# Three selection masks turned by DMA instead of TensorE, and two steps moved forward in their engines' orders

## The chip, the cores and the metric

The kernel runs on one core of one Trainium2 chip. The metric is the device time of one execution in microseconds (us); the time before is the median of three runs, 276.24 us (276.19 to 276.46). Everything else below comes from one profiled execution of the same kernel.

The engines are called by their profile names: PE (TensorE, matmuls), PEld (its weight loads), DVE (VectorE), ACT (ScalarE), POOL (GpSimd) and SP (SyncE, which issues nearly all DMAs; its queue is SPq in the profile).

## The reference

For 4 batches of 8 heads (768 positions, 64 features per head) a block-sparse attention is computed, and its output goes through a two-layer network with a tanh GELU.

```python
k_rep = k.reshape(B, H, n_blocks, block, D).mean(axis=3)          # 12 blocks of 64 keys
gate_scores = np.einsum('bhsd,bhnd->bhsn', q, k_rep)
gate_scores = np.where(causal, gate_scores, -1000000000.0)
top_idx = np.argsort(gate_scores, axis=-1)[..., -top_k:]          # top_k = 3
# a query sees its 3 best key blocks and its own block, and no later position
scores = np.where(mask, scale * (q @ k.T), -1000000000.0)
attn = softmax(scores); attn_out = attn @ v
# x: attn_out as 3072 tokens of 512 features
h = x @ w_in                                                      # 512 -> 2048
g = 0.5 * h * (1.0 + np.tanh(c * (h + 0.044715 * h * h * h)))
out = g @ w_out                                                   # 2048 -> 512
```

## The kernel before

The 32 heads are handled as 16 pairs of heads. Pairs 0 to 3 (batch 0) have their own functions; pairs 4 to 15 go one by one through the steps below. The network runs over 12 chunks of 256 tokens; a chunk needs the attention output of all four pairs of its batch, so the matmuls of earlier batches' chunks are mixed in between the attention of later pairs.

Nothing is scheduled by a planner at build time. A text, `ORDER` (lines 27 to 129), lists 1109 steps by name, and the program calls the function of each in turn. As the whole body stands under `tc.manual_schedule()` (line 162), each engine executes its own instructions in the order in which `ORDER` names them. Between engines, and for buffers that are used again, the framework puts in semaphore waits. So a change of `ORDER` matters only where two steps of the same engine, or two tiles of the same buffer, change places. The names, for pair p (written `x.p.0` with more numbers behind):

- `d.p.x` loads q, k or v (x = 0, 1, 2) by two DMAs on SP; `hn0`, `hn1` (hi_n, line 726) and `ln0`, `ln1` (lo_n, line 736) make the high and low fp16 halves of q and k; the letter behind the colon is the engine (a = ACT, v = DVE, p = POOL).
- `zqh`, `zkh`, `zql` (dma_t, line 746) turn the high q, high k and low q by a DMA transpose on SP; `c0`, `c1` (qk_copy, line 756) copy the turned halves of q and k into the operand tiles `qt` and `kt`, one for each head.
- `s` (k_sum, line 761, PE) sums the keys of each block; `b` (k_block, line 773, DVE, three instructions) makes the gate's weights of it; `g` (gate, line 787, PE) computes the gate scores; `m` (select, line 800, DVE, 14 instructions, the last at line 821) writes for each query and block 0 or a large negative number into `madd16`.
- `mt` (mask_t, line 826) turns that mask on PE: five transposes of 128 by 128 into a PSUM tile. `mc.p.0.hh` (mask_q, line 838) copies 12 rows by 640 columns of it below the q of head hh in `qt`, so that the matmul of the scores adds the mask by itself.
- `k.p.0.i` (score, line 846, PE), `x` (expo, line 859, ACT) and `a` (causal, line 877, POOL) make the six blocks of attention weights; `v` (v_copy, line 770) casts v; `p` (pv, line 887, PE) multiplies by v, and `n` (normalise, DVE, lines 673 and 677) divides.
- `zx` (x_dma, line 900), or `xt` and `xc`, turn the result into `xT`. Then `u` (up, line 947, PE), `y` (gelu, line 964, ACT), `f` (down, line 981, PE), `o` (out_c, line 999) and `w` (out_d, line 1009, a DMA on SP) are the network for a chunk.

The buffers of which the change speaks: PSUM has three wide tiles. The number behind `@` in `ORDER` names the one that a step `u`, `k` or `p` takes; the step waits until the reader of the tile before it (`y`, `x` or `n`) is done. One further PSUM tile, `small`, is shared by `s`, `g`, `mt` and `xt` in turn. In SBUF, the pool `hd` has two buffers of each tag; the tag `ql` holds the turned low q.

Of the kernel before, what the change touches and what calls it, by code (L numbers as in the profile page):

```python
# [27 lines left out]
c.m0.1 c.bi c.ident d0.0.1.0 c.e0 d0.1.0.0 c.ident16 dm24 d0.1.0.1 d0.0.0.0 d0.0.0.1 dd.1.1.0  # L28
dd.1.1.1 d0.1.3.2 d0.0.1.1 t2.0.0@0 c.e.2:a c.v.1 d0.1.1.0 d0.1.1.1 c.gate dm4 c.own r.1.1.0:a
r.1.1.1:a t2.1.1@1 d0.1.0.2 c.cg t2.1.0@2 c.e.1:p h2.0.0 s.0.0 l.0.0 dm8 c.m0.0 c.bd b.0.0 dd.0.1.0  # L30
h2.1.0 s.1.1 c.e.3:p dd.0.1.1 dd.0.2.0 g.0.0 m.0.0 mt.0.0 s.1.0 l.1.0 r.0.1.0:a r.0.1.1:p lw.in.2
c.v.0 h2.1.1 mc.0.0:a dm5 t2.0.1@0 b.1.0 l.1.1 h2.0.1 r.0.2.0:v d0.0.0.2 g.1.0 m.1.0 dm17 mt.1.0
s.0.1 mc.1.0:a dm4 l.0.1 k.0.0.0.0@2 k.0.0.1.0@1 ma.0.0.0 x.0.0.0.0 d0.1.1.2 v.1.0.0:p c.par.0
b.0.1 b.1.1 dm16 d0.0.1.2 x.0.0.1.0 a.0.0.1 g.0.1 k.0.1.0.1@0 k.1.0.0.0@2 k.1.0.1.0@1 ma.1.0.0
x.1.0.0.0 a.0.0.0 lw.out.1 x.1.0.1.0 m.0.1 dd.0.2.1 r.0.2.1:a mt.0.1 mc.0.1:v lw.in.4 g.1.1
k.0.1.1.1@2 v.0.0.1:p lw.in.5 ma.0.1.1 x.0.1.1.1 m.1.1 x.0.1.0.1 t2.0.2@1 d0.0.3.2 s.0.2 h2.0.2
a.0.1.0 dm9 v.0.1.1:a lw.in.3 d0.0.2.2 v.1.1.1:a l.0.2 a.1.0.1 v.1.0.1:p k.1.1.1.0@2 mt.1.1
mc.1.1:v v.0.0.0:p k.1.1.0.0@0 ma.1.1.0 x.1.1.1.0 a.0.1.1 p.0.0.0@1 p.0.0.2 p.0.0.3 p.0.0.1 n.0.0
dm22 d0.1.2.2 cw.in.5:v lw.in.1 v.1.1.0:p dd.1.2.0 cw.in.1:v k.1.1.0.1@2 k.1.1.1.1@1 ma.1.1.1
x.1.1.0.0 a.1.0.0 cw.in.4:v p.1.0.0@0 x.1.1.1.1 d.5.1 dd.1.2.1 dm23 v.0.1.0:p lw.out.0 x.1.1.0.1  # L40
r.1.2.0:a xt.0.0 xc.0.0:a lw.in.0 p.1.0.2 cw.in.2:p d.4.0 p.1.0.3 p.1.0.1 n.1.0 k.0.1.0.0@1
k.0.1.1.0@2 ma.0.1.0 x.0.1.0.0 a.1.1.0 p.1.1.0@0 p.1.1.1 xt.1.0 xc.1.0:v a.1.1.1 p.1.1.2 r.1.2.1:v
lw.out.5 x.0.1.1.0 cw.out.5:p d0.1.5.2 p.0.1.0@1 p.0.1.1 p.1.1.3 n.1.1 cw.in.3:v d.4.1 lw.in.6
lw.in.7 cw.out.1:a hn1.5.0:v p.0.1.3 cw.in.6:p cw.in.7:p lw.out.3 p.0.1.2 t2.1.2@2 n.0.1 s.1.2
b.1.2 xt.1.1 u.0.1.0@0 xc.1.1:a u.0.1.1 y.0.1 hn0.4.0:v xt.0.1 xc.0.1:a b.0.2 u.0.2.0@1 u.0.2.1
y.0.2 u.1.2.0@0 u.1.2.1 y.1.2 u.1.1.0@1 u.1.1.1 ln0.4.0:v zql.4.0 lw.out.2 y.1.1 d0.0.5.2
cw.out.0:a cw.in.0:v u.0.0.0@0 u.0.0.1 g.0.2 u.1.0.0@1 u.1.0.1 y.0.0 hn1.4.0:v u.0.3.0@0 m.0.2
cw.out.3:v mt.0.2 u.0.3.1 h2.1.2 l.1.2 y.1.0 dm9 ln1.4.0:v dm24 y.0.3 cw.out.2:v mc.0.2:v
k.0.2.1.0@2 k.0.2.0.0@1 ma.0.2.0 x.0.2.0.0 g.1.2 d.6.0 hn0.6.0:p x.0.2.1.0 k.0.2.0.1@0 k.0.2.1.1@1
zqh.4.0 ma.0.2.1 x.0.2.0.1 x.0.2.1.1 c.ke.0.0:p ln1.5.0:v m.1.2 mt.1.2 k.0.2.1.2@2 mc.1.2:v s.4.0  # L50
b.4.0 k.0.2.0.2@0 c0.4.0.0:a lw.out.6 ma.0.2.2 f.0.0.0 lw.out.4 lw.out.7 x.0.2.1.2 ln0.6.0:v
cw.out.7:v f.0.0.1 x.0.2.0.2 k.1.2.0.0@1 k.1.2.1.0@2 zkh.5.0 ma.1.2.0 x.1.2.1.0 zqh.6.0 cw.out.6:p
x.1.2.0.0 c.ke.0.1:v cw.out.4:p g.4.0 m.4.0 f.0.0.2 d0.0.4.2 v.0.2.0:v f.0.0.3 o.0.0:a d.5.0
k.1.2.0.1@0 k.1.2.1.1@2 ma.1.2.1 d0.1.4.2 f.0.1.0 hn0.5.0:v ln0.5.0:v x.1.2.0.1 a.0.2.0 zkh.4.0
v.0.2.1:p a.0.2.1 f.0.1.1 p.0.2.0@1 p.0.2.1 c.ke.1.0:a x.1.2.1.1 c0.4.0.1:p mt.4.0 d.6.1 v.1.2.1:p
c1.4.0.0:a mc.4.0.0:v c.par.1 p.0.2.3 p.0.2.2 n.0.2 v.1.2.0:a k.1.2.1.2@0 zqh.5.0 k.1.2.0.2@2
ma.1.2.2 f.0.1.2 x.1.2.0.2 f.0.1.3 zql.5.0 c1.4.0.1:v mc.4.0.1:v x.1.2.1.2 s.5.0 b.5.0 o.0.1:v
k.4.0.1@1 k.4.0.2@2 x.4.0.1 d.4.2 d.5.2 c1.5.0.0:v zql.6.0 a.1.2.0 p.1.2.0@0 p.1.2.1 g.5.0 m.5.0
x.4.0.2 c0.5.0.0:v a.1.2.1 p.1.2.3 c.q0.0 k.4.0.0@1 v.4.0:p f.1.0.0 x.4.0.0 xt.0.2 xc.0.2:a
k.4.0.5@2 p.1.2.2 x.4.0.5 k.4.0.3@1 x.4.0.3 a.4.0.3 hn1.6.0:v d.7.1 ln1.6.0:v a.4.0.5 mt.5.0 d.8.0  # L60
mc.5.0.0:v c0.5.0.1:p zkh.6.0 k.4.0.4@2 f.1.0.1 mc.5.0.1:v n.1.2 c0.6.0.1:v x.4.0.4 u.1.3.0@1
u.1.3.1 y.1.3 s.6.0 f.1.0.2 b.6.0 xt.1.2 w.0.0 xc.1.2:v d.7.0 c1.5.0.1:p hn1.7.0:v ln1.7.0:v
c.ke.1.1:p k.5.0.2@0 k.5.0.1@2 x.5.0.2 k.5.0.3@1 g.6.0 m.6.0 f.1.0.3 u.2.0.0@0 o.1.0:v d.8.1
u.2.0.1 d.9.0 x.5.0.3 a.4.0.4 a.4.0.2 a.4.0.0 a.4.0.1 p.4.0.0@1 x.5.0.1 a.5.0.1 hn0.7.0:v zqh.7.0
mt.6.0 mc.6.0.1:v d.6.2 p.4.0.1 w.1.0 mc.6.0.0:v n.4.0 c1.6.0.0:p y.2.0 c0.6.0.0:p k.5.0.4@2
c1.6.0.1:p f.1.1.0 f.1.1.1 ln0.7.0:v x.5.0.4 c.q0.1 hn1.8.0:v ln1.8.0:v k.5.0.5@1 k.6.0.2@0 x.6.0.2
s.7.0 b.7.0 f.1.1.2 v.5.0:v k.5.0.0@2 c0.7.0.1:v hn0.8.0:p x.5.0.5 ln0.8.0:v x.5.0.0 k.6.0.3@0
a.5.0.0 zql.7.0 zkh.7.0 zqh.8.0 s.8.0 f.1.1.3 b.8.0 x.6.0.3 o.1.1:a a.6.0.3 w.1.1 k.6.0.4@1 w.0.1
x.6.0.4 u.2.1.0@2 u.2.2.0@0 u.2.2.1 y.2.2 hn0.9.0:p g.7.0 a.5.0.4 u.2.1.1 c0.7.0.0:v y.2.1
u.2.3.0@1 m.7.0 a.6.0.4 u.2.3.1 mt.7.0 zql.8.0 y.2.3 a.5.0.2 ln0.9.0:v a.5.0.3 a.5.0.5 p.5.0.0@0  # L70
p.5.0.1 mc.7.0.0:v k.6.0.1@2 f.2.0.0 f.2.0.1 x.6.0.1 v.6.0:v d.10.0 a.6.0.1 n.5.0 k.6.0.0@1
k.6.0.5@2 f.2.0.2 c1.7.0.1:v x.6.0.5 a.6.0.5 x.6.0.0 mc.7.0.1:v c1.7.0.0:v k.7.0.5@0 k.7.0.2@2
zkh.8.0 x.7.0.5 c1.8.0.1:p g.8.0 x.7.0.2 hn0.10.0:v m.8.0 d.7.2 a.6.0.0 a.6.0.2 f.2.0.3 o.2.0:a
k.7.0.3@1 x.7.0.3 a.7.0.3 zx.5.0 c0.8.0.0:a k.7.0.0@0 p.6.0.0@2 p.6.0.1 x.7.0.0 mt.8.0 k.7.0.4@1
x.7.0.4 n.6.0 f.2.1.0 mc.8.0.0:v k.7.0.1@0 f.2.1.1 a.7.0.2 a.7.0.4 mc.8.0.1:a zx.4.0 c0.8.0.1:v
c1.8.0.0:v k.8.0.3@1 d.9.1 zqh.9.0 d.10.1 d.8.2 zql.9.0 a.7.0.0 d.11.0 x.7.0.1 a.7.0.1 v.7.0:v
k.8.0.1@2 x.8.0.1 a.7.0.5 x.8.0.3 xt.6.0 xc.6.0:v p.7.0.0@0 p.7.0.1 n.7.0 hn1.9.0:a zkh.9.0
c1.9.0.0:p hn1.10.0:v ln0.10.0:v zql.10.0 f.2.1.2 f.2.1.3 w.2.0 k.8.0.5@2 xt.7.0 x.8.0.5 k.8.0.4@1
xc.7.0:a zqh.10.0 k.8.0.2@0 u.3.3.0@2 u.3.3.1 ln1.9.0:v x.8.0.4 s.9.0 x.8.0.2 a.8.0.2 u.3.2.0@1
u.3.2.1 v.8.0:v u.4.2.0@0 u.4.2.1 b.9.0 g.9.0 ln1.10.0:v d.11.2 zkh.10.0 y.3.3 o.2.1:a y.3.2 y.4.2  # L80
d.12.0 hn0.11.0:v ln0.11.0:v a.8.0.4 u.3.0.0@2 zql.11.0 u.3.1.0@1 u.3.0.1 y.3.0 k.8.0.0@0 m.9.0
mt.9.0 mc.9.0.0:v mc.9.0.1:v u.3.1.1 u.5.1.0@2 u.5.1.1 y.3.1 d.11.1 y.5.1 s.10.0 a.8.0.5 x.8.0.0
c1.9.0.1:v c0.9.0.1:p c0.9.0.0:v k.9.0.1@1 x.9.0.1 hn0.12.0:a c1.10.0.0:v f.3.0.0 f.3.0.1 f.3.0.2
f.3.0.3 d.15.2 a.8.0.0 k.9.0.3@2 b.10.0 g.10.0 c1.10.0.1:p k.9.0.4@0 d.13.1 d.9.2 x.9.0.3 d.15.0
a.8.0.3 x.9.0.4 a.8.0.1 p.8.0.0@1 o.3.0:v m.10.0 p.8.0.1 n.8.0 u.4.0.0@2 u.4.0.1 y.4.0 k.9.0.2@0
x.9.0.2 ln0.12.0:v a.9.0.2 f.3.1.0 hn1.13.0:v ln1.13.0:v k.9.0.5@1 zqh.11.0 mt.10.0 mc.10.0.1:a
a.9.0.1 u.5.0.0@2 x.9.0.5 a.9.0.5 c0.10.0.0:v f.3.1.1 f.3.1.2 f.3.1.3 hn1.11.0:v k.9.0.0@0
mc.10.0.0:v o.3.1:a d.12.1 ln1.11.0:v x.9.0.0 a.9.0.0 u.4.1.0@1 zkh.11.0 v.9.0:v u.4.1.1 y.4.1
zx.8.0 s.11.0 a.9.0.4 c1.11.0.1:p u.4.3.0@0 u.4.3.1 d.14.2 y.4.3 a.9.0.3 u.5.0.1 y.5.0 hn0.15.0:p
b.11.0 w.2.1 c0.10.0.1:v d.10.2 zqh.12.0 g.11.0 k.10.0.3@1 x.10.0.3 f.4.0.0 k.10.0.1@0 x.10.0.1  # L90
c1.11.0.0:v k.10.0.5@2 m.11.0 f.4.0.1 hn1.12.0:v zkh.12.0 f.4.0.2 p.9.0.0@1 a.10.0.3 ln0.15.0:v
p.9.0.1 n.9.0 mt.11.0 k.10.0.4@0 x.10.0.4 d.13.0 mc.11.0.1:v mc.11.0.0:a f.4.0.3 v.11.0:v
c0.11.0.1:p u.5.2.0@1 ln1.12.0:v k.10.0.2@0 o.4.0:a x.10.0.5 u.5.2.1 k.10.0.0@2 x.10.0.2 zql.12.0
s.12.0 w.4.0 u.5.3.0@0 u.5.3.1 a.10.0.5 y.5.2 y.5.3 a.10.0.2 c1.12.0.0:a f.4.1.0 c0.11.0.0:p
v.10.0:v k.11.0.0@1 f.4.1.1 a.10.0.4 b.12.0 g.12.0 f.4.1.2 f.4.1.3 hn0.13.0:v x.10.0.0 a.10.0.0
x.11.0.0 d.12.2 k.11.0.1@0 x.11.0.1 k.11.0.2@2 m.12.0 mt.12.0 zx.9.0 c0.12.0.1:v o.4.1:v x.11.0.2
a.10.0.1 p.10.0.0@1 ln0.13.0:v p.10.0.1 n.10.0 zqh.13.0 c1.12.0.1:v f.5.0.0 k.11.0.3@0 zkh.13.0
k.11.0.4@2 c0.12.0.0:v v.14.0:a d.13.2 k.11.0.5@1 f.5.0.1 x.11.0.3 a.11.0.0 f.5.0.2 zql.13.0
# [985 lines left out]
```

## Time and profile before

| | |
|---|---|
| median of three runs | 276.24 us |
| the profiled execution | 278.32 us, of which 276.6 us are the span from its first to its last instruction |
| granted TensorE clock | 0.994 |
| busy, PE | 263.3 us, 95% of the span |
| busy, ACT / DVE / POOL | 198.2 / 141.4 / 86.9 us |
| transposes of masks on PE (line 830) | 60 for pairs 4 to 15, 219 ns each, overlapping |
| DMA transposes on SP (lines 751 and 903) | 36 + 8 |

Two things are needed to read it. Matmuls overlap, so the distance from one start to the next is shorter than the duration of one: what PE spends on a group is best read from the start of that group to the start of the next. And the profile shows an idle time only where no work of the engine is recorded; as the matmul before still counts as busy for a moment, a wait of PE can be some 0.15 us longer than the idle time given.

### The profile page before, as it was taken

Reading aid. Unit: us, or ns where it says so; the run is one execution under the profiler, and the core shown is the slowest. Engines: PE = TensorE matmul, PEld = TensorE weight load, DVE = VectorE, ACT = ScalarE, POOL = GpSimd, SP = SyncE. Lnnn points to the kernel's source line nnn. Section 1 sums busy time; section 2 is a strip of 40 time slices with the busy share of each in tenths; the row PEclk is TensorE's granted clock in tenths of the full one; section 3 lists DMA queues with packets and bytes.
Section 4 is the critical chain, followed back from the end, with each engine's and each line's share of the span. In section 5 each row is a group of like instructions: output and inputs, shape, how many; then the busy total and the mean of one; then the engine's idle time right before and its main releaser. Section 6 shows DMA issues by size and latency. Waiting matters only on the chain.

```text
span 276.6 us, 6874 instructions
## 1 busy us (share of the span) xinstructions
PE 263.3 (95%) x2785; PEld 183.1 (66%) x2785; DVE 141.4 (51%) x442; ACT 198.2 (72%) x229; POOL 86.9 (31%) x159
## 2 busy tenths in 40 slices
...
GB/s 173 279 329 282 252 270 295 276 170 180 175 248 192 177 199 190 185 200 213 148 212 118 188 119 114 101 135 157 79 7 23 97 0 2 0 76 2 76 92 138
DMA packets 114416, 42.66 MB, mean 154 GB/s; under 512 B 102992, under 2 KB 107344, under 8 KB 114384
## 3 DMA queue, kind: packets, MB, share of 16 engines
...
q8 instruction: 22, 0.36, 0.7%
q14 instruction: 10, 0.08, 0.1%
...
## 4 chain that ended last, share of the span: by engine, by line
PE 70%; DVE 8%; DMA 7%; ACT 7%; issue 4%; POOL 2%; SPq 1%; POOLq 0%; ACTq 0%
PE hps L957 23%; PE ops L993 20%; PE st L852 7%; PE pv L894 4%; DMA io<-in_k_dram 4%; PE pso L993 3%; PE dm L1032 3%; ACT at L868 2%; DMA qhT<-hn 2%; DMA io<-in_q_dram 2%; PE st L598 2%; DVE ln L739 2%; ACT L868 1%; PE pv L662 1%; PE st L616 1%
## 5 line engine op out<-in xcount | busy, mean ns | idle before, releaser
L957 PE MATMUL hps<-xT,w_in 128*128 128x256 f16 x768 | 90.1, 272 | 0.0
L957 PEld LDWEIGHTS <-w_in 128*128 128x128 f16 x768 | 74.0, 98 | 12.5 <-DVE xn L677 0.2
L993 PE MATMUL ops<-w_out,gT 128*128 128x512 f16 (+1 forms) x352 | 81.9, 371 | 0.0
L868 ACT ACTIVATE at<-st 128x1024 f16<-128x1024 f32 (+1 forms) x72 | 62.8, 918 | 11.1 <-PE st L852 10.8
L967 ACT ACTIVATE gT<-hps 128x1024 f16<-128x1024 f32 x48 | 48.1, 1024 | 23.0 <-PE hps L957 22.8
L993 PEld LDWEIGHTS <-gT 128*128 128x128 f16 x400 | 37.0, 97 | 36.2 <-issue 0.5
L882 POOL TENSOR_SCALAR_AFFINE_SELECT at<-at 128x256 f16<-128x256 f16 x72 | 31.1, 451 | 76.4 <-ACT at L868 66.6
L852 PE MATMUL st<-qk 76*128 76x128 f16 (+2 forms) x192 | 35.6, 306 | 0.5 <-ACT at L868 0.5
L739 DVE SCALAR_TENSOR_TENSOR ln<-io,hn 128x768 f16<-128x768 f32 x24 | 25.3, 1059 | 0.3
L635 ACT ACTIVATE at<-st 128x768 f16<-128x768 f32 (+1 forms) x24 | 20.7, 913 | 6.5 <-PE st L616 4.9
L852 PEld LDWEIGHTS <-qk 76*128 76x128 f16 x192 | 16.5, 97 | 10.8 <-issue 0.9
L1006 DVE COPY w_o<-pso 128x512 f32<-128x512 f32 x1 | 0.7, 692 | 36.9 <-PE pso L993 36.9
L894 PEld LDWEIGHTS <-at 128*128 128x128 f16 x504 | 17.1, 97 | 2.5 <-issue 0.6
L894 PE MATMUL pv<-v,at 128*128 128x65 f16 x504 | 17.7, 193 | 0.6 <-POOL v L771 0.6
L1006 ACT COPY osb<-ops 128x512 f32<-128x512 f32 (+1 forms) x13 | 7.3, 562 | 14.8 <-PE ops L993 12.8
L187 POOL TENSOR_SCALAR hn<-io 128x768 f16<-128x768 f32 x6 | 13.0, 2160 | 9.2 <-PE hps L957 5.1
L1032 PE MATMUL dm<-zsrc 128*128 128x512 f16 (+3 forms) x45 | 13.4, 431 | 2.0 <-POOL zsrc L235 2.0
L673 DVE RECIPROCAL zrec<-pv 128x12 f32<-128x12 f32 x12 | 2.8, 232 | 22.6 <-PE pv L894 22.4
L967 ACT ACT_TABLE_LOAD x11 | 14.1, 1283 | 0.2
L839 DVE COPY qk<-mt 12x640 f16<-12x640 f16 x19 | 9.2, 485 | 7.9 <-ACT qk L839 4.3
L648 POOL TENSOR_SCALAR_AFFINE_SELECT at<-at 128x512 f16<-128x512 f16 x12 | 7.8, 661 | 17.3 <-ACT at L635 17.1
L868 ACT ACT_TABLE_LOAD x9 | 11.5, 1283 | 2.2 <-PE st L852 2.0
...
## 6 DMA issues: line engine op xcount, KB each, us to landing
...
```

The lines of the kernel that those rows point to most:

```text
L187: math_on[eng].tensor_scalar(out=out, in0=in_, scalar1=c, scalar2=None, op0=ALU.mult)
L635: nc.scalar.activation(out=ov, in_=iv, func=AF.Exp, bias=0.0, scale=SCALE / (QS * QS))
L739: math_on[eng].scalar_tensor_tensor(out=g.rearrange("p t c -> p (t c)"), in0=IO[p, x].rearrange("p t h d -> p (t h d)"), scalar=QS, in1=U[ ...
L839: copy_on[eng](out=qt[p % 2][hh][64:64 + NBLK, 128:], in_=U["mt", p][64 * hh:64 * hh + NBLK, 0:S - 128])
L852: nc.tensor.matmul(st[:, hh, cb:cb + nq * 128], kt[p % 2][hh][0:64 + NBLK, jc * 128:(jc + 1) * 128], qt[p % 2][hh][0:64 + NBLK, qc * 128:( ...
L868: nc.scalar.activation(out=ov, in_=iv, func=AF.Exp, bias=0.0, scale=SCALE / (QS * QS))
L882: nc.gpsimd.affine_select(out=a, in_=a, compare_op=ALU.is_ge, fill=0.0, base=0, pattern=[[0, 2], [1, 128]], channel_multiplier=-1,)
L894: nc.tensor.matmul(U["pv", p][:, o:o + 65], AT[p, hh, jc, qc], v16[p % NSLOT][:, jc, hh, :], start=(jc == 0), stop=(jc == qc),)
L957: nc.tensor.matmul(hps[:, j * TCH:(j + 1) * TCH], w_in16[:, ci, fi * 128:(fi + 1) * 128], xT[:, ci, t0:t0 + TCH], start=(ci == 0), stop=(c ...
L967: nc.scalar.activation(out=g.rearrange("p a w -> p (a w)"), in_=G["h", ch, dj], func=AF.Gelu_apprx_tanh, bias=0.0, scale=1.0,)
L993: nc.tensor.matmul(G["o", ch, ti][:, a:b], G["g", ch, dj][:, j, row * 128:(row + 1) * 128], w_out16[:, fi, a:b], start=(fi == 0), stop=(fi ...
L1032: nc.tensor.matmul(U["dm"][:, 0:m * 128].rearrange("p (a x) -> p a x", a=m), zsrc, zsrc.unsqueeze(1).to_broadcast([128, m, 128]), start=Tr ...
```

## The change

For pairs 13, 14 and 15 the step `mt` is replaced by `zm` (mask_dma): one DMA transpose, issued by SP, that writes the turned mask into SBUF, into a buffer of the tag `ql`. The copies `mc` of these pairs read it from there. For the other pairs nothing changes.

```diff
+    def mask_dma(p):
+        mt = hd.tile([128, S - 128], FP16, tag="ql", name=f"mt_{p}")
+        nc.sync.dma_start_transpose(
+            out=mt.rearrange("d (t p) -> d t p", p=128),
+            in_=madd16[p % 2][:, 2:2 * NC].rearrange("p a b -> p (a b)"))
+        U["mt", p] = mt
...
-        step(f"mt.{un}", mask_t, p)
+        if p in (13, 14, 15):
+            step(f"zm.{un}", mask_dma, p)
+        else:
+            step(f"mt.{un}", mask_t, p)
```

`ORDER` is written anew as a whole. Taken apart by engine, these are all the differences (in each row, the old order of the neighbours and the new one):

```diff
 PE    (mt.13.0, mt.14.0 and mt.15.0 left out)
 SP
-  d.15.1 zqh.14.0 zql.15.0 zql.14.0 w.3.0 zkh.15.0 zqh.15.0 w.5.1 w.6.0 w.3.1 zx.13.0
+  d.15.1 zm.13.0 zqh.14.0 zql.15.0 zql.14.0 w.3.0 zkh.15.0 zqh.15.0 w.5.1 zm.14.0 w.6.0 w.3.1 zm.15.0 zx.13.0
 DVE
-  ln0.7.0 hn1.8.0 ln1.8.0 b.7.0 v.5.0
+  ln0.7.0 b.7.0 hn1.8.0 ln1.8.0 v.5.0
-  m.13.0 ln1.14.0 mc.13.0.0 ln0.14.0 b.14.0
+  m.13.0 ln1.14.0 ln0.14.0 mc.13.0.0 b.14.0
 POOL
-  a.12.0.0 c0.14.0.0 a.12.0.5 v.12.0 c1.14.0.1
+  a.12.0.0 v.12.0 c0.14.0.0 a.12.0.5 c1.14.0.1
 ACT
-  y.6.0 mc.13.0.1 hn1.15.0 c0.14.0.1 y.6.1
+  y.6.0 hn1.15.0 mc.13.0.1 c0.14.0.1 y.6.1
-  o.6.1 x.14.0.1 x.14.0.2 mc.15.0.1
+  o.6.1 mc.15.0.1 x.14.0.1 x.14.0.2
```

The wide PSUM tiles are numbered anew from pair 5 on. For most steps that is a change of name alone: the tile waits for the same reader as before. For these the tile before it is another one (in brackets):

```diff
-  k.5.0.5 (p.4)     k.6.0.2 (u.2.0)     k.6.0.5 (k.6.0.1)   k.7.0.5 (p.5)       k.7.0.1 (k.7.0.0)
+  k.5.0.5 (u.2.0)   k.6.0.2 (p.4)       k.6.0.5 (p.5)       k.7.0.5 (k.6.0.1)   k.7.0.1 (p.6)
-  k.5.0.2 (p.1.2)   k.5.0.1 (k.4.0.4)   k.8.0.3 (k.7.0.4)   k.8.0.1 (p.6)       k.13.0.1 (p.12)     k.13.0.4 (u.6.3)
+  k.5.0.2 (k.4.0.4) k.5.0.1 (p.1.2)     k.8.0.3 (k.7.0.0)   k.8.0.1 (k.7.0.4)   k.13.0.1 (u.6.3)    k.13.0.4 (p.12)
-  k.14.0.1 (k.14.0.5)  k.14.0.2 (k.14.0.3)  k.15.0.5 (k.14.0.1)  k.15.0.0 (k.14.0.2)  k.15.0.3 (p.13)
+  k.14.0.1 (p.13)      k.14.0.2 (k.14.0.5)  k.15.0.5 (k.14.0.3)  k.15.0.0 (k.14.0.1)  k.15.0.3 (k.14.0.2)
```

More of the change, by code (lines that the diff above doesn't have):

```diff
@@ L27 @@
 ORDER = """
[L28 to L98, printed above, removed]
@@ new lines @@
+x.1.1.1.1 lw.out.5 x.1.1.0.1 d0.1.5.2 xt.0.0 r.1.2.0:a p.1.0.2 p.1.0.3 a.1.1.0 p.1.0.1 k.0.1.0.0@1
+xc.0.0:a n.1.0 k.0.1.1.0@2 a.1.1.1 ma.0.1.0 x.0.1.0.0 p.1.1.0@0 p.1.1.1 xt.1.0 p.1.1.2 x.0.1.1.0
+xc.1.0:v p.0.1.0@1 p.0.1.1 r.1.2.1:v p.1.1.3 d.4.1 cw.out.1:a n.1.1 p.0.1.3 p.0.1.2 t2.1.2@2
+cw.in.3:v lw.in.6 xt.1.1 hn1.5.0:v u.0.1.0@0 xc.1.1:a n.0.1 u.0.1.1 s.1.2 lw.in.7 cw.out.5:p xt.0.1
+b.1.2 u.0.2.0@1 lw.out.3 y.0.1 u.0.2.1 xc.0.1:a hn0.4.0:v b.0.2 u.1.2.0@0 y.0.2 ln0.4.0:v u.1.2.1
+cw.in.0:v zql.4.0 u.1.1.0@1 hn1.4.0:v y.1.2 cw.in.6:p u.1.1.1 lw.out.2 d0.0.5.2 cw.in.7:p u.0.0.0@0
```

124 lines of the change are left out of this document (94 added, 30 removed).

## The prediction

> **What bounds the kernel now.** I read the busy times first, then what PE waited for, then the chain of waits that ended last, then each engine's order in time around the three masks.
>
> ```profile
> span 276.6 us, 6874 instructions
> PE 263.3 (95%) x2785; PEld 183.1 (66%) x2785; DVE 141.4 (51%) x442; ACT 198.2 (72%) x229; POOL 86.9 (31%) x159
> ...
> q8 instruction: 22, 0.36, 0.7%
> ...
> PE kp L765 <- DVE kbd L775: 0.6, 1, 0.6
> PE pv L894 <- POOL v L771: 0.6, 1, 0.6
> ```
>
> PE works 95% of the span, so nearly everywhere a microsecond is saved only where PE gets less to do or waits less. PE's own waits are few, and the change touches three of them: 0.6 us before a key sum (kp), 0.6 us before a product with v (pv), and one behind ACT that is shown further below. The two named are pair 8's `s`, which needs the tile `small` back from `b.7`, and pair 12's `p`. The last parts of the chain, in order of time:
>
> ```profile
> 180.91 5.19 DMA qhT<-hn
> 187.42 0.80 POOL v L771
> ...
> 197.75 0.28 PE mt L830 x5
> ...
> 199.77 0.43 PE st L852 x2
> ...
> 207.02 0.28 PE mt L830 x5
> ```
>
> So up to 188 us the chain does not run through PE but through the transpose of pair 14's high q, and `mt.13`, at 181.74, is not on it. `mt.14` and `mt.15` are on it with 0.28 us each. From 188 us on the chain is PE's to the end, but for one short wait behind ACT in between, which follows PE's own shift.
>
> **The change part by part.** *Masks 14 and 15 off PE.* Ten matmuls and ten weight loads go, 2 x 0.28 = 0.56 us, if the masks come in time by DMA.
>
> ```profile
> 192.67 0.22 DVE L821 TENSOR_TENSOR madd<-lt,ownm 128x120 f16<-128x120 f16 x1
> 198.06 0.98 DVE L839 COPY qk<-mt 12x640 f16<-12x640 f16 x2 [0.48 <-PE mt L830]
> ...
> 202.30 0.22 DVE L821 TENSOR_TENSOR madd<-lt,ownm 128x120 f16<-128x120 f16 x1
> 209.21 0.68 ACT L839 COPY qk<-mt 12x640 f16<-12x640 f16 x1
> 210.16 1.15 PE L852 MATMUL st<-qk 76*128 76x128 f16 x8
> ...
> DMA to landing us min/median/max: 2.7/2.8/3.7
> DMA to landing us min/median/max: 2.7/3.7/8.8
> ```
>
> The first landing row is that of the transposes of line 903, the second that of line 751. Mask 14 is ready at 192.89 and could land at 195.7; its copies run at 198.06, and the scores that need them at 199.8, so even the line 751 median of 3.7 leaves over a microsecond. Mask 15 is ready at 202.52 and lands near 205.4. `mc.15.0.1` now goes before two exponentials on ACT and makes them 0.68 us later at most; the last of them then ends near 209.85, and the scores that take its buffer come some 0.5 us behind 210.16: hidden. On SP, `w.6.0`, `w.3.1` and `zx.13` stand behind the new transposes; all three wait for later work anyway. I take the gain as -0.56 (bounds -0.56 and -0.28, if one of the two meets a new wait).
>
> *Mask 13 off PE, and its transpose ahead of `zqh.14` on SP.* This is the part with a price.
>
> ```profile
> 179.35 1.16 SPq L423 DMA_DIRECT2D io<-in_k_dram  x2
> 180.91 1.22 SPq L751 DMA_TRANSPOSE qhT<-hn  x1
> 182.22 4.23 SPq L751 DMA_TRANSPOSE qlT<-ln  x2
> 179.75 0.22 DVE L821 TENSOR_TENSOR madd<-lt,ownm 128x120 f16<-128x120 f16 x1
> 181.74 0.44 PE L830 MATMUL mt<-ident,madd 128*128 128x128 f16 x5
> 182.02 5.41 PE L957 MATMUL hps<-xT,w_in 128*128 128x256 f16 x48
> 182.99 0.68 ACT L839 COPY qk<-mt 12x640 f16<-12x640 f16 x1
> 186.18 0.83 ACT L758 COPY qk<-qhT 64x768 f16<-64x768 f16 x1 [1.64 <-DMA qhT<-hn]
> 187.03 2.85 ACT L967 ACTIVATE gT<-hps 128x1024 f16<-128x1024 f32 x3
> 187.54 0.16 PE L765 MATMUL kp<-blockind,ln 128*128 128x2 f16 x1
> 188.26 1.44 PE L894 MATMUL pv<-v,at 128*128 128x65 f16 x42 [0.56 <-POOL v L771]
> 184.25:186.00 1.75, 1.75 (x19) 1.57 (x17) 0.93 (x1) 0.29 (x1) 0.00 (x0) 1.00 0.21 17
> ```
>
> Before, `zqh.14` issued at 180.91, when `hn0.14` on POOL was done, and landed 5.19 us later, at 186.10. Only then could ACT do `c0.14.0.1` and behind it the GELU `y.6.1` (about 1.0 us), which frees the PSUM tile that `p.12` takes; POOL did `c0.14.0.0` first too and `v.12` after it (to 188.22). So the two ends, v.12 at 188.22 and y.6.1 at 188.0, let `p.12` start at 188.26, while PE had issued its last kp matmul at 187.54 and could have gone on at 187.56: a true wait of 0.70 us. Moving `v.12` up takes away only the later of two ends: by itself 0.15 us. With qhT landing at L, `p.12` starts at L + 0.93 + 1.0 + 0.06, about L + 2.0. PE now comes there at 187.28, as it has 0.28 us less to do, but that only lengthens its wait.
>
> After: SP is free at 180.51 and the mask is ready at 179.97, so `zm.13` issues at 180.6 and holds SP for 1.22 us; `zqh.14` issues at 181.87, 0.96 us later than before. At the undisturbed 2.75 us it would land at 184.6. But before, the DMA engines moved almost nothing from 184.25 to 186.00 (17 GB/s; the columns end with DMA share and GB/s), and qhT landed as that ended. I read this as an instruction fetch: q8 has 22 packets with 0.36 MB, 16 KB each, and 5570 instructions of PE and PEld over 22 are 253 per packet. If so, the standstill is tied to a place in PE's instruction stream. Ten instructions less put it ten later in the work, 5 x 5.41/48 = 0.56 us, less the 0.28 us saved: 0.28 us later, to 186.28. The new qhT would still be under way at its beginning and land as it ends, L = 186.4, and `p.12` starts at 188.4: +0.1 against before. Bounds: -0.98 (no standstill in the way, L = 184.6, PE not waiting at all) and +1.1 (L = 187.4, a landing 1.0 us later, the spread of the line 903 row). I take +0.1, as qhT's own row is the nearest.
>
> [...]
>
> `mc.13` reads SBUF instead of PSUM, which no row shows; I take the 0.68 us that it has on ACT. From a landing near 183.5 even twice that ends by 185 and thus before qhT. `hn1.15` before it and `ln0.14` before its DVE twin fill time in which these engines waited: nothing. `zql.14` now needs its buffer back from both `mc.13`, at about 184.8; it issued after 185.2 before: nothing. `s.14` and `g.15` lose a wait for `small` that never was the last: nothing.
>
> *`b.7` ahead of `hn1.8` and `ln1.8`.* Pair 8's sum needs these two as well.
>
> ```profile
> 85.09 2.13 POOL L187 TENSOR_SCALAR hn<-io 128x768 f16<-128x768 f32 x1
> 86.65 0.98 DVE L187 TENSOR_SCALAR hn<-io 128x768 f16<-128x768 f32 x1
> 87.66 0.96 DVE L739 SCALAR_TENSOR_TENSOR ln<-io,hn 128x768 f16<-128x768 f32 x1
> 88.54 0.17 DVE L775 TENSOR_TENSOR kbd<-kp,bdsmall 128x24 f32<-128x24 f32 x1
> 88.77 0.44 PE kp L765 x12
> 89.20 0.55 DVE L771 CAST v<-io 128x768 f16<-128x768 f32 x1
> ...
> 100.02 0.54 DVE L187 TENSOR_SCALAR hn<-io 128x768 f16<-128x768 f32 x1
> ```
>
> Before, the sum started 0.05 us behind the end of the first instruction of `b.7`, 88.71, and `ln1.8` had ended at 88.62. After, the three instructions of `b.7` (88.54 to 89.20, 0.66 us) come first, and the sum waits for `ln1.8`. `hn1.8` took 0.98 us beside POOL's `hn0.8`, which ends at 87.22, against 0.54 us elsewhere; behind `b.7` it runs after that end. So `b.7` 86.65 to 87.46 (0.66, and some 0.15 that POOL may hold it), `hn1.8` to 88.04, `ln1.8` from 87.96 to 88.92, sum at 88.97: +0.20. The wait changes its name. Bounds: 0 (`b.7` wholly in the time that `hn1.8` lost to POOL) and +0.66.
>
> *The PSUM tiles numbered anew.* I went through the list; one entry matters.
>
> ```profile
> 97.89 0.96 DVE L677 TENSOR_TENSOR xn<-pv,zrec 128x768 f16<-128x768 f32 x1
> 99.40 1.02 ACT L868 ACTIVATE at<-st 128x1024 f16<-128x1024 f32 x1
> 99.59 0.60 PE L852 MATMUL st<-qk 76*128 76x512 f16 x2
> 100.47 0.27 PE L852 MATMUL st<-qk 76*128 76x128 f16 x2 [0.29 <-ACT at L868]
> ```
>
> `k.6.0.5` waited for the exponential of `k.6.0.1`, to 100.42. Two 512-wide matmuls take 0.43 us (199.77 row), so PE could have gone on at 100.02: a wait of 0.45 us. Its new tile waits for `n.5`, done at 98.85. What is late next is `k.7.0.5`, which inherits the exponential, but PE comes there only at 101.0. So -0.45 (bounds -0.45 and 0). All later work up to 188 us is ordered by semaphores behind PE and shifts with it.
>
> Sum: -0.56 + 0.10 + 0.20 - 0.45 = -0.71 us against the profiled execution's own 278.32 (span 276.6 and 1.7 around it). The median of the runs is 276.24, 2.1 lower; the same difference gives 275.5.
>
> **The rivals.** *qhT escapes the standstill.* It issues later and the fetch too; if the fetch falls elsewhere or stops nothing, L = 184.6, and the term +0.10 becomes -0.98: 274.5. For it: most transposes land in under 4 us. Against it: before, the undisturbed 2.75 us would have ended at 183.7, over half a microsecond ahead of the standstill, and it was caught; now they end at 184.6, and the standstill begins at 184.5.
>
> *qhT lands a microsecond behind the standstill.* The second row from SP, two low-q transposes, spent 4.23 us in the same standstill. Then the term is +1.1, the sum +0.3: 276.5.
>
> *`zm.13` is itself held in the standstill.* It lands at 186.4, and ACT does its 0.68 us copy behind that: `p.12` at 189.05, term +0.79, sum 0: 276.2. Against it: it issues 3.6 us ahead.
>
> *The mask is late, and the kernel slower.* If `zm.13` lands at Z, ACT does `mc.13.0.1`, `c0.14.0.1` and `y.6.1` one after the other, and `p.12` starts at Z + 0.1 + 0.68 + 0.83 + 1.0 + 0.06, Z + 2.67. The sum is zero at `p.12` = 189.07, Z = 186.4, and slower by 0.2% from Z = 186.95, 6.35 us after the issue. The slowest transpose of line 751 took 8.8; half way, 7.6, Z = 188.2, gives +1.8: 278.0. Against it: qhT's 5.19 has the standstill in it already, and `zm.13` starts earlier.
>
> [...]
>
> **How the numbers follow.** 0.2% is 0.55 us, about what a measurement of this kernel can tell. Forecast 0.47 (275.5), qhT free 0.13 (274.5), qhT later 0.17 (276.5), `zm.13` held 0.08 (276.2), mask late 0.15 (278.0). Faster: 0.13 and six sevenths of the forecast, as -0.71 is close to the bound, 0.53. Slower: 0.15 and a third of "qhT later", 0.20. Within: 0.27. The range 274.4 to 277.0 holds the first four and the cheap end of the last; the forecast's own is 275.1 to 275.9.
>
> **What would show it.** Right: transposes of line 830 down to 45; PE's wait before pv stays, now behind ACT's gT; its wait before kp stays, behind ln instead of kbd; none before `k.6.0.5`. Wrong: no wait before pv, or one above 1.5 us; a wait of PE for a mask copy after 190 us; a qhT landing more than 6.4 us after its issue; a sum of pair 8 after 89.3.

## The result

The changed kernel is slower: 278.67 us against 276.65 (medians of 22 runs each), a ratio of 1.0064 with a 95% interval of 1.0041 to 1.0087, so +1.77 us (+1.1 to +2.4). The forecast was 275.5, from a median of three runs of the kernel before (276.24) that the 22 runs put 0.4 us higher. Yet the two profiled executions have the same span, 276.5 and 276.6 us, and their parts differ a good deal. The page of the changed kernel:

```profile
span 276.5 us, 6850 instructions
PE 263.3 (95%) x2770; PEld 182.7 (66%) x2770; DVE 137.3 (50%) x442; ACT 198.4 (72%) x229; POOL 88.2 (32%) x159
...
q8 instruction: 21, 0.34, 0.5%
```

PE does 15 matmuls less and is as busy as before. Below, times of a step are starts on PE. The shift of a step is its start in one profile less its start in the profile of the kernel before; where the shift falls or rises, PE has won or lost that time. First what the change was about, the masks, from the view of the tile `mt`:

```profile
L829 PE MATMUL mt<-ident,madd x45: 217/219/222, 65.7 to 162.1; 128*128 128x128 f16 x45
...
L845 ACT COPY qk<-mt x5: 680/684/721, 108.6 to 207.3; 12x640 f16<-12x640 f16 x5
L839 SPq DMA_TRANSPOSE mt<-madd x3: 1200/1200/1202, 180.8 to 202.5; - x3
...
  DMA mt<-madd: 0.8, 1
...
DMA to landing us min/median/max: 2.5/2.6/2.6
```

45 transposes of masks are left on PE, and the three on SP land 2.6 us after their issue. One copy, pair 13's on DVE, stood 0.8 us for a landing; no PE wait stands behind one. The shift falls by 0.28 us at each of `mt.13`, `mt.14` and `mt.15`, and rises by 0.10 at `f.7.0.0`, for which I have no explanation. `k.6.0.5` runs on without a wait (it is the second pair of these four matmuls): -0.45 us.

```profile
101.22 0.71 PE L858 MATMUL st<-qk 76*128 76x512 f16 x4
```

What cost the time lies some 130 us ahead of the first mask that was changed. The timeline of ACT and of PE around 52 us, first in the kernel before, then in the changed one (start, duration, and in brackets the idle time before and who ended it):

```profile
50.01 1.02 ACT L967 ACTIVATE gT<-hps 128x1024 f16<-128x1024 f32 x1 [0.83 <-PE hps L957]
51.05 1.28 ACT L635 ACT_TABLE_LOAD   x1
52.66 3.83 ACT L635 ACTIVATE at<-st 128x1024 f16<-128x1024 f32 x4 [0.33 <-PE st L616]
...
52.23 0.40 PE L616 MATMUL st<-mrow,E 12*128 12x256 f16 x8
...
53.74 0.39 PE L598 MATMUL st<-qk 64*128 64x256 f16 x4 [0.20 <-ACT at L635]
```

```profile
51.30 1.28 ACT L634 ACT_TABLE_LOAD   x1 [1.67 <-PE st L615]
52.59 3.83 ACT L634 ACTIVATE at<-st 128x1024 f16<-128x1024 f32 x4
...
50.82 0.40 PE L615 MATMUL st<-mrow,E 12*128 12x256 f16 x8
...
53.67 0.39 PE L597 MATMUL st<-qk 64*128 64x256 f16 x4 [1.54 <-ACT at L634]
```

Between the GELUs and the exponentials ACT loads another table, 1.28 us. Before, it did so while PE still made the scores, and the first exponential followed the scores at once. After, ACT sat idle for 1.67 us until the scores were there and loaded the table only then. So PE, which here came 1.4 us earlier than in the other profile, got nothing of it: it waited 1.54 us instead of 0.20, and the shift rises by 1.34. Its early arrival is not the reason: in the profiles of t5, t6 and t10, below, PE comes as early and stands idle there for 0.20 us.

And PE paid twice. The next view cuts time into stretches, here first of the changed kernel and then of the kernel before (length, busy time of PE, PEld, DVE, ACT and POOL with the number of instructions; the last three columns are PEclk, the granted clock as a share of full speed, then DMA share and GB/s):

```profile
24.00:31.00 7.00, 5.59 (x80) 3.15 (x78) 4.51 (x9) 5.63 (x9) 5.20 (x10) 1.00 0.90 260
...
52.00:55.00 3.00, 1.40 (x23) 0.60 (x19) 1.11 (x10) 2.99 (x4) 2.71 (x3) 1.00 1.13 297
55.00:59.00 4.00, 3.87 (x31) 1.68 (x31) 2.38 (x6) 3.53 (x5) 0.39 (x1) 0.57 1.30 243
```

```profile
24.00:31.00 7.00, 5.59 (x56) 2.59 (x55) 4.07 (x7) 4.13 (x6) 4.58 (x9) 0.76 0.96 260
...
52.00:55.00 3.00, 2.80 (x53) 1.47 (x50) 1.25 (x10) 2.67 (x4) 1.03 (x2) 1.00 0.94 316
55.00:59.00 4.00, 3.80 (x52) 1.93 (x53) 2.95 (x6) 3.61 (x5) 3.18 (x3) 1.00 1.41 137
```

In the changed kernel the granted clock drops to 0.57 in the four microseconds behind the wait, and the shift rises by another 1.48 between `ma.0.2.1` and `k.1.2.0.0`, at 54.0 and 59.4 us. The kernel before had such a drop too in its profile, at 24 to 31 us (0.76). So the two profiled spans show one drop each, and the rest nearly cancels: +1.34 for the table load, -0.70 at `p.12` (see below) and -0.96 for all the other parts of the change. Over all runs it is not so. A drop, some 3.4 us at half the clock (0.57 over 4 us and 0.76 over 7 are 1.7 us lost each), takes 0.006 off a run's mean clock, and I count drops by that: a mean of 0.990 or lower is two, 0.997 or more is none, and one lies between. Of the 22 runs of the changed kernel 15 had two, 6 had one and 1 had none, 1.64 drops per run; in 89 runs of the kernel before, taken with the experiments, it was 6, 44 and 39, or 0.63. The medians of these 39, 44 and 6 runs are 276.25, 277.49 and 279.60 us; the changed kernel's one run without a drop took 276.80. What a drop costs depends on its place. t7's profile, further below, has one at 8 to 12 us, where PE waits for loads, and lost nothing by it (its shift at 17 us is +0.05):

```profile
5.00:10.00 5.00, 2.75 (x16) 2.40 (x17) 1.06 (x4) 2.07 (x3) 2.78 (x7) 0.86 1.26 251
10.00:15.00 5.00, 4.13 (x33) 3.23 (x32) 4.00 (x18) 2.62 (x4) 1.05 (x4) 0.80 1.20 297
```

One drop more per run, at up to 1.48 us, is most of the difference; the table load's +1.34 is mostly paid for by what the change wins elsewhere, 0.96 us.

**Why the table load moved.** The listing of the built program's instructions on ACT, with what each waits for (`r` copies a loaded tile into a float32 staging tile; `x.0.1.0.0` and the like are exponentials of batch 0):

```
                              kernel before          changed kernel
r.1.2.0  (copy into w32)      a DMA, POOL            two DMAs, DVE
x.0.1.0.0                     PE                     PE, POOL
x.0.1.1.0                     PE, ACT                PE, ACT, POOL
table load before x.0.2.0.0   -                      PE
x.0.2.0.0 (exponential)       PE                     POOL
```

ACT's order is the same in both. But `ORDER` is one list, and its order across the engines also decides which buffer of a shared set each new tile gets. The seven float32 staging tiles (tag `w32`) are shared by the loads on SP (`lw` loads weights) and the `r` copies on ACT and DVE. As the list was written anew, four loads on SP (`lw.in.0`, `d.4.0`, `lw.out.5`, `d0.1.5.2`) stand ahead of `r.1.2.0` instead of behind it, and `r.1.2.0` gets another buffer. Before, it waited for POOL. As I read it, ACT thereby knew that POOL was past the selects in question, and the exponentials needed no wait for POOL of their own. After, `x.0.2.0.0` needs two waits; the first stands ahead of it, and the table load comes between the two. (In t3, below, where the load is done earlier, both waits stand with `x.0.2.0.0`.)

### The profile page after: what moved, and what is told of

It reads as the page before. It is cut to its first block, busy times and chain, and to the rows that moved or that the text cites. A ratio compares the mean times of both kernels' runs of the same rounds, so it can differ in the third digit from the quotient of the medians.

```text
span 276.5 us, 6850 instructions
## 1 busy us (share of the span) xinstructions
PE 263.3 (95%) x2770; PEld 182.7 (66%) x2770; DVE 137.3 (50%) x442; ACT 198.4 (72%) x229; POOL 88.2 (32%) x159
## 4 chain that ended last, share of the span: by engine, by line
PE 77%; DVE 8%; ACT 5%; DMA 5%; issue 3%; SPq 1%; POOL 0%; ACTq 0%
PE hps L966 28%; PE ops L1002 23%; PE st L858 7%; PE pv L900 5%; PE pso L1002 3%; DMA io<-in_k_dram 3%; PE dm L1041 2%; DMA io<-in_q_dram 2%; DVE ln L738 2%; ACT at L874 2%; PE st L597 1%; PE pv L661 1%; PE st L615 1%; ACT at L634 1%; DVE hn L186 1%
## 5 line engine op out<-in xcount | busy, mean ns | idle before, releaser
L1002 PE MATMUL ops<-w_out,gT 128*128 128x512 f16 (+1 forms) x352 | 83.1, 375 | 0.0
L738 DVE SCALAR_TENSOR_TENSOR ln<-io,hn 128x768 f16<-128x768 f32 x24 | 23.8, 999 | 0.3
L186 POOL TENSOR_SCALAR hn<-io 128x768 f16<-128x768 f32 x6 | 14.1, 2351 | 7.3 <-DMA io<-in_q_dram 5.5
L1041 PE MATMUL dm<-zsrc 128*128 128x512 f16 (+3 forms) x45 | 12.3, 400 | 2.0 <-POOL zsrc L234 2.0
L676 DVE TENSOR_TENSOR xn<-pv,zrec 128x768 f16<-128x768 f32 x12 | 11.5, 957 | 0.4
```

Source lines behind the costliest of these rows:

```text
L186: math_on[eng].tensor_scalar(out=out, in0=in_, scalar1=c, scalar2=None, op0=ALU.mult)
L676: nc.vector.tensor_tensor(out=xn[:, 0:nt].rearrange("p c h d -> p h c d"), in0=pz[:, :, :, 0:64], in1=zrec[:, :, 0:nt].unsqueeze(3).to_bro ...
L738: math_on[eng].scalar_tensor_tensor(out=g.rearrange("p t c -> p (t c)"), in0=IO[p, x].rearrange("p t h d -> p (t h d)"), scalar=QS, in1=U[ ...
L1002: nc.tensor.matmul(G["o", ch, ti][:, a:b], G["g", ch, dj][:, j, row * 128:(row + 1) * 128], w_out16[:, fi, a:b], start=(fi == 0), stop=(fi ...
L1041: nc.tensor.matmul(U["dm"][:, 0:m * 128].rearrange("p (a x) -> p a x", a=m), zsrc, zsrc.unsqueeze(1).to_broadcast([128, m, 128]), start=Tr ...
```

## The experiments

**The staging buffers, undone and done alone.** The first kernel is the changed one with the four loads behind `r.1.2.0` in the list; the second is the kernel before with them ahead of it. No engine's order changes in either.

```diff
 (t1_after_w32: the changed kernel's list, and t2_before_w32 the other way round)
- ... lw.in.0 ... d.4.0 ... lw.out.5 ... d0.1.5.2 xt.0.0 r.1.2.0:a
+ ... xt.0.0 r.1.2.0:a lw.in.0 d.4.0 lw.out.5 d0.1.5.2
```

> The changed kernel with four loads (lw.in.0, d.4.0, lw.out.5, d0.1.5.2) written behind r.1.2.0 in the list, as they stood before; no engine's order changes, but the float32 staging buffers rotate as before, and the load of the exponential's table on ACT is again free of the wait for PE that it carries in the changed kernel. Theory A (the table load, 1.28 us, moved behind the scores by a second wait of x.0.2.0.0, and the slow clock after the 1.54 us wait of PE, cost what the kernel lost): the wait before the second scores of unit (0,2) falls from 1.54 to about 0.2 us, and the time to 0.4 to 0.9 us under the kernel before. Theory B (the late part costs it: masks, v.12, b.7): the time stays at that of the changed kernel, some 2 us over the kernel before. Theory C (the clock alone, by chance): about 1 us over it, the wait unchanged.

> The kernel before with the same four loads written ahead of r.1.2.0, as in the changed kernel; nothing else. Theory A: PE waits some 1.5 us before the second scores of unit (0,2), the table load starts behind the scores, and the time rises by 1.3 us, or by 2.7 us where the clock falls behind that wait. Theory B: no change, within 0.3 us. Theory C: no change in the wait; the clock is as in the kernel before.

ACT's table load and PE's second scores in t2, and then ACT's table load in t1:

```profile
51.12 1.28 ACT L633 ACT_TABLE_LOAD   x1 [1.67 <-PE st L614]
...
53.49 0.39 PE L596 MATMUL st<-qk 64*128 64x256 f16 x4 [1.54 <-ACT at L633]
```

```profile
51.03 1.28 ACT L633 ACT_TABLE_LOAD   x1
52.64 1.94 ACT L633 ACTIVATE at<-st 128x1024 f16<-128x1024 f32 x2 [0.33 <-PE st L614]
```

Measured against the kernel before: t1 0.9983 (0.9951 to 1.0015), t2 1.0079 (1.0042 to 1.0117), +2.2 us. The listing of t2's instructions up to 60 us shows the changed kernel's waits, that of t1 the kernel before's. Four entries moved in a list cost as much as the whole change lost, and taking them back takes the loss away: theory A; B and C fall. Whether t1 is also faster than the kernel before, its interval doesn't say. t1's profile has a span of 275.0, 1.6 under the kernel before, with the same early drop of the clock; its shift changes by +0.23 up to `s.8`, -0.45 at `k.6.0.5`, -0.28 at `mt.13`, -0.70 at `p.12`, -0.28 and -0.28 at the other masks and +0.10 at `f.7.0.0`.

**The table load by itself, and the wait filled.** The buffers stay as in the changed kernel.

```diff
 (t3_after_preload)
+        if (g, c, j, i) == (0, 2, 0, 0):
+            nc.scalar.activation(out=scr, in_=bdsmall[:, 0, 0:1],
+                                 func=AF.Exp, bias=0.0, scale=1.0)
 (t4_after_fill; dm28 stands for seven matmuls of zeros)
- x.0.2.1.0 k.0.2.1.1@1
+ x.0.2.1.0 dm28 k.0.2.1.1@1
```

> The changed kernel with one exponential of a 128x1 column ahead of x.0.2.0.0 on ACT, which takes the table load ahead of the wait for PE; the buffers stay as in the changed kernel. Theory A: as with the four loads moved back, 0.3 to 0.9 us under the kernel before (the small exponential costs ACT some 0.2 us in a stretch in which it is idle). If instead the other buffers of the staging loads cost the time (later loads of w_out), it stays at the changed kernel's time.

> The changed kernel with seven matmuls of zeros (512 wide, some 0.22 us each) on PE ahead of k.0.2.1.1, in the time in which PE waits 1.54 us for ACT; the table load stays where it is. If the slow clock from 55.7 to 58.6 us (0.50 of full speed) follows from that idle time, the granted clock stays at 1.00 there and the kernel wins some 1.4 us of what it lost: about 0.6 us over the kernel before. If the slow clock is independent of it, the time stays at that of the changed kernel or rises by up to 0.1 us.

t3: 0.9966 (0.9942 to 0.9989), -0.94 us. In its profile the load starts at 49.43, right behind the GELU, and PE stands idle for 0.26 us ahead of the second scores. So it is the place of the table load, and not the later loads of `w_out` that wait for other buffers. t4: 1.0019 (0.9995 to 1.0044), +0.5 us. There PE still can't go on before the late exponential, but is busy with matmuls of zeros, and the clock stays up:

```profile
52.00:55.00 3.00, 3.00 (x36) 1.21 (x32) 0.98 (x9) 2.99 (x4) 2.87 (x3) 1.00 1.04 374
55.00:59.00 4.00, 3.79 (x50) 1.98 (x52) 3.27 (x7) 3.99 (x5) 1.90 (x2) 1.00 1.22 264
```

None of t4's 12 runs has a mean clock of 0.990 or lower, against 15 of 22 without the fill and 4 of 8 in t2: the drop at 55 us comes of PE's idle time there. (Six of t4's runs have one drop; its place is not known.)

**The move of b.7, and the mask of pair 13.** Both start from t1.

```diff
 (t5_b7_back, DVE's order)
- ln0.7.0 b.7.0 hn1.8.0 ln1.8.0 v.5.0
+ ln0.7.0 hn1.8.0 ln1.8.0 b.7.0 v.5.0
 (t6_mt13, PE's order; zm.13.0 is gone from SP's)
- u.6.0.1 u.8.0.0
+ u.6.0.1 mt.13.0 u.8.0.0
```

> As the run with the four loads moved back, and in DVE's order hn1.8 and ln1.8 go ahead of b.7 again, as in the kernel before. If the move of b.7 costs 0.24 us of PE's time at pair 8's sum (in the profile of the four-loads run PE's start there changed by -0.72 and then by +0.98 against the kernel before, with -0.02 around it), PE's wait behind ln disappears, the one behind kbd comes back with 0.6 us, and the profile's ledger against the kernel before shows no net change at s.8: 0.24 us less in all. If the end of v.5 or of the selects behind it set the time instead, nothing is won.

> As the run with the four loads moved back, but the mask of pair 13 is turned on PE again (mt.13 ahead of u.8.0.0, its transpose on SP gone); v.12, hn1.15 and ln0.14 stay where the change put them. If the place of qhT_14's landing against the instruction fetch decides p.12, and zm.13 only delays it, the ledger rises by 0.28 us at mt.13 and stays 0 or gains at p.12 (qhT_14 issues up to 1.2 us earlier, and so is the less likely to be under way at the fetch): +0.28 against the four-loads run. If moving v.12 forward had been what removed the wait of p.12, p.12 starts without a wait whatever qhT_14 does.

t5: 0.9986 (0.9956 to 1.0015). The rows of DVE and PE at pair 8's sum, in the changed kernel and in t5:

```profile
88.05 0.17 DVE L774 TENSOR_TENSOR kbd<-kp,bdsmall 128x24 f32<-128x24 f32 x1
...
88.80 0.56 DVE L186 TENSOR_SCALAR hn<-io 128x768 f16<-128x768 f32 x1
89.39 0.96 DVE L738 SCALAR_TENSOR_TENSOR ln<-io,hn 128x768 f16<-128x768 f32 x1
...
89.42 0.18 PE L764 MATMUL kp<-blockind,hn 128*128 128x2 f16 x1
90.41 0.18 PE L764 MATMUL kp<-blockind,ln 128*128 128x2 f16 x1 [0.82 <-DVE ln L738]
```

```profile
86.89 0.98 DVE L185 TENSOR_SCALAR hn<-io 128x768 f16<-128x768 f32 x1
87.90 0.96 DVE L737 SCALAR_TENSOR_TENSOR ln<-io,hn 128x768 f16<-128x768 f32 x1
88.78 0.18 DVE L773 TENSOR_TENSOR kbd<-kp,bdsmall 128x24 f32<-128x24 f32 x1
...
89.01 0.16 PE L763 MATMUL kp<-blockind,hn 128*128 128x2 f16 x1 [0.69 <-DVE kbd L773]
```

With `b.7` first the sum starts without a wait, as `hn1.8` is just done, and stops at the second matmul until `ln1.8` is nearly done, 0.82 us; the shift rises by 0.23 from ahead of `k.5.0.5` to the end of `s.8` (0.22 or 0.23 in four of the five profiles with the move, 0.45 in t6, and 0 to 0.03 in the six without it). In t6 another wait comes in: `k.6.0.2` takes the tile of `p.4` by the new numbers, and PE stood 0.68 us until DVE's `n.4` was done:

```profile
84.67 0.59 PE L857 MATMUL st<-qk 76*128 76x512 f16 x2 [0.68 <-DVE xn L675]
```

But t5's ratio to the kernel before is no better than t1's: in its profile, in which the clock did not drop, PE waited elsewhere for 1.63 us, at `f.0.0.2` for a cast of the weights on POOL.

```profile
59.37 1.89 PE L1001 MATMUL ops<-w_out,gT 128*128 128x512 f16 x8 [1.63 <-POOL w_out L352]
```

The profiles of t7 and t9 have such a wait there too, 0.30 and 0.76 us, those of t3, t6 and t10 none; and none of the five has a drop of the clock at 24 to 62 us. So what PE wins ahead of 58 us can be lost to the cast of the weights; how often that happens in runs without a profile is not known.

t6: 1.0004 (0.9967 to 1.0041), no worse than t1 beyond the intervals. In the profile the 0.28 us at `mt.13` come back, and `p.12` starts without a wait, as in t1.

**p.12, or what the wait of 0.70 us was.** Here the runs say together what no single one says. The profile of the kernel before has a wait ahead of `p.12`; of the eleven others only t3's has one. Rows of SP, ACT and PE, of t3 and then of the changed kernel:

```profile
178.60 1.20 SPq L842 DMA_TRANSPOSE mt<-madd  x1
179.89 1.23 SPq L753 DMA_TRANSPOSE qhT<-hn  x1
...
184.51 0.83 ACT L760 COPY qk<-qhT 64x768 f16<-64x768 f16 x1 [1.65 <-DMA qhT<-hn]
...
186.40 1.44 PE L903 MATMUL pv<-v,at 128*128 128x65 f16 x42 [0.80 <-ACT gT L979]
```

```profile
180.85 1.20 SPq L839 DMA_TRANSPOSE mt<-madd  x1
182.15 1.23 SPq L750 DMA_TRANSPOSE qhT<-hn  x1
...
185.65 0.83 ACT L757 COPY qk<-qhT 64x768 f16<-64x768 f16 x1
...
188.47 1.44 PE L900 MATMUL pv<-v,at 128*128 128x65 f16 x42
```

In t3 the transpose of qhT landed at 184.43, 4.54 us after its issue; ACT stood 1.65 us for it and PE 0.80 behind the GELU. In the changed kernel it landed in 2.84 us, and nobody waited. Both have `zm.13` and `v.12` in their new places. t2, t7 and t10 have no `zm.13` and `v.12` in its old place, and no wait either (qhT landed after 2.74, 3.13 and 3.14 us). In t3 and in the kernel before, the packet of the fetch started with qhT still under way, 2.47 and 3.34 us after its issue, and qhT landed about 2 us behind that start. In eight of the other profiles it had landed by then. But in t4 and t8 the fetch also started while it was under way, 2.26 and 2.25 us after its issue, and it landed after 2.84 and 2.85 us as if undisturbed. So the fetch is a part of it at most; what else delays qhT, and why it was still under way after 3.34 us in the kernel before, stays open. The change isn't what decides it.

**The numbering of the PSUM tiles alone.**

```diff
 (t7_slots: the kernel before's list, with the wide tiles' numbers of the changed one)
- k.6.0.0@1 k.6.0.5@2      k.7.0.5@0
+ k.6.0.0@2 k.6.0.5@0      k.7.0.5@1      (and so on; 74 numbers in all)
```

> The kernel before with the changed kernel's numbers of the wide PSUM tiles and nothing else. If the numbering is worth what PE waited before k.6.0.5, that wait of 0.45 us is gone, k.7.0.5 starts without one, and the ledger ends 0.4 to 0.5 us lower, except where PE's earlier arrival at p.12 is eaten by the wait for qhT_14. If the wait only goes on to k.7.0.5 the ledger ends level.

0.9995 (0.9968 to 1.0023). The profile shows -0.45 at `k.6.0.5`, no wait at `k.7.0.5`, and no other change above 0.2 us from 60 us up to `p.12`; in the times 0.45 us is within the interval. `p.12` starts without a wait here too, with `v.12` where it always was.

**A version that beats both, and the other clock drop.** t9 is t3 with `hn1.8` and `ln1.8` ahead of `b.7` again. t8 is t5 with seven matmuls of zeros ahead of `ma.1.1.0`, where PE stands idle for 1.41 us in every other kernel (a wait of some 1.57); t10 is the kernel before with these alone.

```diff
 (t8_best, t10_before_fill)
- ma.1.1.0
+ dm28 ma.1.1.0
```

> The changed kernel with the small exponential ahead of x.0.2.0.0 (as in the run with the early table load) and with hn1.8 and ln1.8 ahead of b.7 again. From the ledger: masks -0.84, their way back at f.7.0.0 +0.10, the numbering of the PSUM tiles -0.45, nothing at s.8: -1.2 us of PE's time against the kernel before, and 0.24 less than the run with the early table load, whose median was 0.34% under the kernel before: 0.35 to 0.45% under it. If the move of b.7 is worth nothing outside the profile, 0.34% stays.

> The run with the four loads and b.7 moved back, and seven matmuls of zeros ahead of ma.1.1.0, where PE waits 1.57 us for mrow at 24.5 us in all kernels. If such a wait is what halves the clock a microsecond or two later (granted 0.50 at 27 to 29 us in the profile of the kernel before), the clock stays at 1.00 in nearly all runs, and the median falls below that of the run without the fill by up to 1.3 us, some 1.9 us or 0.7% under the kernel before. If the clock falls without regard to it, nothing is won, and up to 0.2 us lost.

> The kernel before with seven matmuls of zeros on PE ahead of ma.1.1.0, in the 1.57 us for which PE waits for mrow at 24.5 us; nothing else. If that wait brings the slow clock at 27 us, which is in the profile of the kernel before and of the four-loads run, the mean granted clock is 1.00 in nearly all its runs (of the runs of the kernel before so far, about half are at 0.994 or lower) and the median falls by up to 1 us. If not, as many runs as before are at 0.994, and the median stays within 0.3 us.

t9: 0.9951 (0.9924 to 0.9977), -1.36 us: the lowest ratio of all. It and t3 are the two whose intervals lie wholly under the kernel before; between the two nothing is shown. t8: 0.9978 (0.9949 to 1.0006), with 7 of 12 runs at a clock of 0.997 or more, against 4 of t5's 12. t10: 0.9993 (0.9966 to 1.0021), with 8 of 12 runs at a clock of 1.00 (0.997 or more) against 10 of 23 of the kernel before beside it. Both were expected to have nearly all runs at 1.00 and missed it, and neither ratio shows that this fill helps. And t8's profile has a drop at 55 us without a long wait ahead of it (from 52 to 55 us PE is busy for 2.60 of the 3):

```profile
55.00:56.00 1.00, 1.00 (x4) 0.36 (x3) 0.97 (x3) 1.00 (x2) 1.00 (x2) 0.50 1.28 289
```

So idle time is one cause of the drop; what else brings it stays open.

## Why the prediction was wrong

**The step that failed** is the inventory: "The PSUM tiles numbered anew. I went through the list; one entry matters". The list renumbers the staging tiles in SBUF as well, and the prediction had no term for that and none at all ahead of 85 us. It compared each engine's order, found the first 60 us unchanged and took that for no change. The missing terms are +1.34 for the table load and some +1.48 for one more drop of the clock per run.

The account for the changed kernel closes with the terms as measured; the wait of 0.70 us ahead of `p.12` is left out of it, as all but two profiles lack it. Masks 3 x -0.28 and +0.10, numbering -0.45, `b.7` +0.23: -0.96. With the table load +1.34: +0.38. With 1.64 - 0.63 = 1.0 drops more, were each at a place where it costs 1.48: +1.9 (measured +1.77). For t2, which has the table load alone and 1.38 drops per run, 1.34 + 0.75 x 1.48 = +2.4 (measured +2.2, +1.2 to +3.2). For t3 -0.96 (measured -0.94), for t4, in which the load is late and the clock stays up, +0.38 (measured +0.5), and for t9, without the move of `b.7`, -1.2 (measured -1.36). It doesn't close so well for the kernels with the four loads moved back: t1 -0.96 (measured -0.5), t5 and t8 -1.2 (measured -0.4 and -0.6), t6 -0.7 (measured +0.1). Each sum lies within its interval, but all four fall short by 0.5 to 0.8 us; PE's wait for the cast of the weights in t5 and its wait for `n.4` in t6 could be a part of that, and the rest is open.

**Masks 14 and 15, -0.56: right.** -0.28 each in every profile that has them. Its cover was right too: PE waited for no landing.

**`b.7`, +0.20: right**, +0.23. The wait behind `kbd` became one behind `ln`, as said; the stop came one matmul later than I had it, as the first needs `hn1.8` alone.

**PSUM numbering, -0.45: right**, to the hundredth, and `k.7.0.5` had no wait. That only one entry mattered is not quite so: `k.6.0.2` behind `p.4` cost PE a wait of 0.68 us in t6, and none in the other profiles.

**`zm.13` and `p.12`, +0.10: wrong as a model.** It took one execution's collision for the rule. Without it mask 13 is worth -0.28 like the others. Of the signs named, "no wait before pv" came true against the forecast, as in the rival "qhT escapes the standstill", but that rival's whole -0.98 isn't the change's either: t2, t7 and t10, whose orders there are those of the kernel before, have no such wait to lose. That the fetch sits at a place in PE's instructions held roughly (in the trace of the kernel before, 195 to 332 instructions of PE and PEld start between two of q8's packets, 251 in the median), but ten instructions are not 0.28 us. In the time of the kernel before (the packet's start less the shift of PE there) it came at 184.25 in the kernel before, at 184.4 to 184.7 in the five profiles whose PE has ten instructions less up to there, and at 183.5 in t4 and t8, which have four more. But t2, t6 and t7, with as many as the kernel before, had it at 183.96, 183.55 and 184.24, and t10, with fourteen more, at 183.42. The copy of the mask from SBUF, for which no row stood, took ACT 0.72 us for pair 13, against the 0.68 taken.

**The rivals.** None had the mechanism. "The mask is late, and the kernel slower" gave 278.0, close to the result by luck, for a reason that didn't occur: the slowest landing of a mask in the eight profiles that have one was 3.33 us.

**The own time of the profile.** That 278.32 stood 2.1 us over the median was carried over as an offset. It was a sign: a drop of the clock at 27 us lay in it, and a median can move by how often such drops occur.
